# The last product of the last block split by token tile, its output stored in four pieces

## The chip, the cores and the metric

The kernel runs on one core of a Trainium2 chip. The metric is the device time of one execution in microseconds, as the median of several executions. A core has five engines that run side by side and wait for each other by semaphores: PE (TensorE, matrix products, which go to the accumulation memory PSUM), DVE (VectorE, elementwise), ACT (ScalarE, functions and copies), POOL (GpSimd) and SP (SyncE, which here issues the DMA transfers).

## The reference, cut to what matters

The kernel computes a state-space attention block (Mamba-2 SSD, 4 sequences of 768 tokens, 8 heads of 32) and a gated feed-forward network behind it:

```
def _moe_ref(x, w_gate, w_val, w_out, rms_g):      # x: 3072 tokens x 256
    rms = np.sqrt(np.mean(x * x, axis=-1, keepdims=True) + 1e-06)
    xn = x / rms * rms_g
    g = xn @ w_gate                                # 256 x 1536
    silu = g * (1.0 / (1.0 + np.exp(-g)))
    val = xn @ w_val                               # 256 x 1536
    return (silu * val @ w_out).astype(np.float32) # 1536 x 256
```

Its `x` is the attention output, with the heads side by side. The change concerns the last product alone, `silu * val @ w_out`, for the last 512 tokens.

## The kernel before, in words

All is float32. The 3072 tokens go in six blocks of 512 (`TB`, `NBLK`). Blocks 1 to 5 take each matrix product of the network in a Strassen (Winograd) form with seven products of half-size matrices instead of eight. The order of all steps of a block is written out by hand as a list of names with numbers (the strings at the end of the kernel); a loop calls the function of each name. There is one list for block 1, one for blocks 2 to 4 and one for the last block, in which nothing of a next block is prepared. The engines keep the order of this list, each for its own instructions, and wait for each other where data or buffers ask for it.

The output product of a block has a left matrix of 512 tokens x 1536, held turned as six tiles `h` (`j` = 0 to 5, each with two slices of 128 hidden units), and `w_out`. The tokens are split in two halves (`a` = 0, 1) of two token tiles (`t` = 0, 1) of 128 each, in the order that `put_half` shows (`(t a p)`), the 256 output columns in two halves of 128 (`m` = 0, 1). The steps are:

- `O.k.j` (`product_o`, L801 to L817): product k of tile j, two 128x128 matmuls, one per token tile, at L815. Products 1, 6 and 7 add up in one bank, products 5 and 3 in a second, 2 in a third, 4 in a fourth. Products 2 and 5 are in tiles of the tag "val", the others in tiles of the tag "gate", two buffers each. A tile holds both token tiles side by side.
- `s`, `s2`, `s3`, `s4` (L786 to L798): sums and differences of tiles of h on DVE; `s4.j` (L798) makes the left matrix of product 3, `Sh[j]`.
- `Otake.k` (`taken_o`, L827): ACT copies the first bank to the tile `v` after products 1, 6 and 7.
- `Oadd.c` (`total_o`, L829 to L834): DVE adds such a copy and one of the other banks into quarter c of the output tile `ob` (first digit: token half, second: column half). `Oadd.22` reads the second bank when product 5 is in it, `Oadd.12` when product 3 has been added as well.
- `out.a` (`put_half`, L836 to L838): SP stores one token half, 256 rows of 256 columns.

In the last block the list ends with product 3 (`O.3.0` to `O.3.5`), `Oadd.21`, `out.1`, `Oadd.12` and `out.0`: the last store waits for the last addition, and that for the last matmul.

Of the kernel before, what the change touches and what calls it, by code (L numbers as in the profile page):

```python
# [9 lines left out]
FP32 = mybir.dt.float32  # L10
# [5 lines left out]
ALU = mybir.AluOpType  # L16
# [4 lines left out]
def kernel(  # L21
# [33 lines left out]
    nc = tc.nc  # L55

    P = 128
# [5 lines left out]
    DM, DF = moe_w_gate.shape  # L63
    T = NB * S
    NF = DF // P
    NPAIR = T // 256
    TB = 512
    NT = TB // P
    NBLK = T // TB
# [11 lines left out]
    def bank(name, shape):  # L81
        return mm.tile(list(shape), FP32, tag="one", bufs=2, name=name)
# [5 lines left out]
    pairs, later, sides = {}, {}, ("left", "right")  # L88
# [29 lines left out]
    wo = const.tile([P, NF, DM], FP32, name="wo")  # L118
# [573 lines left out]
    def combine_w(j):  # L692
        if j < NF // 4:
            s = raw.tile([P, 2, 4, P], FP32, tag="wr", name="sw", bufs=6)
        else:
            s = const.tile([P, 2, 4, P], FP32, name="sw%d" % j)
        Sw[j] = s
        f1, f2 = slice(2 * j * P, (2 * j + 1) * P), slice((2 * j + 1) * P, (2 * j + 2) * P)
        a11, a12, a21, a22 = wgv[:, :, 0, f1], wgv[:, :, 1, f1], wgv[:, :, 0, f2], wgv[:, :, 1, f2]
        for k, in0, in1, op in ((0, a21, a22, ALU.add), (1, s[:, :, 0], a11, ALU.subtract),  # L700
                                (2, a11, a21, ALU.subtract), (3, a12, s[:, :, 1], ALU.subtract)):
            nc.vector.tensor_tensor(out=s[:, :, k], in0=in0, in1=in1, op=op)
# [66 lines left out]
    two = {}  # L769
# [30 lines left out]

    Os, ts, obs = {}, {}, {}  # L801

    def product_o(blk, k, j):
        bank_of = {1: "X", 6: "X", 7: "X", 2: 2, 4: 4, 5: 5, 3: 5}[k]
        if k in (1, 2, 4, 5) and j == 0:
            val = k in (2, 5)
            Os[bank_of] = later[val].tile([P, 512], FP32, tag="val" if val else "gate",
                                          name="o", bufs=2)
        o = Os[bank_of]
        a11, a12, a21, a22 = tiles_of_h(blk, j)  # L810
        lhsT = {1: a11, 2: a12, 4: a22, 7: a21}[k] if k in (1, 2, 4, 7) else Sh[j]
        rhs = {1: wo[:, 2 * j, 0:P], 2: wo[:, 2 * j + 1, 0:P], 3: wo[:, 2 * j + 1, P:DM],
               **{k: two[j // 2][:, {4: 3, 5: 0, 6: 1, 7: 2}[k], j % 2] for k in (4, 5, 6, 7)}}[k]
        for t in range(2):
            nc.tensor.matmul(out=o[:, t * P:(t + 1) * P], lhsT=lhsT[:, t], rhs=rhs,  # L815
                             start=(k in (1, 2, 4, 5) and j == 0 and t == 0), stop=True,
                             skip_group_check=True)  # L817

    def halves_of(o):
        return o[:, 0:2 * P].rearrange("p (t m) -> p t m", t=2)  # L820
# [5 lines left out]
            ts[k] = ffn.tile([P, 2, P], FP32, tag="v", name="v", bufs=2)  # L826
        nc.scalar.copy(out=ts[k], in_=halves_of(Os["X"]))  # L827

    def total_o(blk, c):  # L829
        if blk not in obs:  # L830
            obs[blk] = ffn.tile([P, 2, 2, DM], FP32, tag="ob", name="ob", bufs=1)
        a, m, v, o = {11: (0, 0, 1, 2), 22: (1, 1, 7, 5), 21: (1, 0, 7, 4), 12: (0, 1, 6, 5)}[c]
        nc.vector.tensor_tensor(out=obs[blk][:, :, a, m * P:(m + 1) * P], in0=ts[v],
                                in1=halves_of(Os[o]), op=ALU.add)  # L834

    def put_half(blk, a):  # L836
        dst = out[blk * TB:(blk + 1) * TB, :].rearrange("(t a p) m -> p t a m", t=2, a=2)
        nc.sync.dma_start(out=dst[:, :, a], in_=obs[blk][:, :, a])  # L838

    def put(blk, k, o, ob):  # L840
        nc.scalar.copy(out=ob, in_=o)
# [154 lines left out]
    def of_chunk(n, fn):  # L996
# [3 lines left out]
        "P": product_gv, "take": taken_gv, "C": total_gv, "silu": silu_gv, "hid": hide_gv,  # L1000
        "s": combine_h, "s3": difference_h, "s2": second_h, "s4": fourth_h,
        "O": product_o, "Otake": taken_o, "Oadd": total_o, "out": put_half,
        "cw": lambda blk, j: combine_w(j) if blk == 1 else None,
        "two": lambda blk, j: combine_wo(j) if blk == 1 else None,
        "turn": of_pair(1, turn), "T": of_pair(1, lambda p, i: turned(p, i, ac.copy)),
# [14 lines left out]
    for blk in range(1, NBLK):  # L1020
# [27 lines left out]
        elif blk < NBLK - 1:  # L1048
            order = """
                P.1.0 load.0 take.1.0 turn.0.1 P.1.1 take.1.1 spread.0 P.6.0 P.2.0 T.0.1  # L1050
                turn.0.0 take.6.0 P.6.1 Tt.0.1.0 Tt.0.1.1 take.6.1 T.0.0 P.7.0 C.11.0 Tt.0.0.0
                P.2.1 P.7.1 take.7.0 C.11.1 P.4.0 P.5.0 Tt.0.0.1 take.7.1 P.4.1 silu.21.0 C.22.0
                silu.21.1 silu.11.1 g.0 silu.22.0 P.5.1 scale.1 hid.21.1 silu.11.0 hid.11.0
                hid.21.0 P.3.0 C.22.1 hid.11.1 P.1.3 L1.0.3 P.1.2 take.1.3 P.3.1 hid.22.0 A.0
                turn.1.1 take.1.2 T.1.1 P.2.2 L1.0.2 P.6.2 P.6.3 C.12.0 C.12.1 L.0 take.6.2 S.0
                P.2.3 take.6.3 C.11.3 turn.1.0 P.7.3 silu.22.1 P.7.2 Tt.1.1.0 silu.12.0 hid.12.0
                hid.22.1 y.0 C.11.2 T.1.0 take.7.3 take.7.2 spread.1 P.5.2 sq.0 silu.12.1 P.5.3
                silu.11.2 hid.12.1 silu.11.3 P.4.3 silu.21.3 C.22.2 Tt.1.1.1 Tt.1.0.0 yt.0
                C.22.3 P.4.2 s.0 hid.21.3 Tt.1.0.1 P.3.2 P.1.5 silu.21.2 hid.11.3 P.3.3 sub.0
                g.1 take.1.5 P.6.5 hid.11.2 silu.22.2 s.1 take.6.5 P.1.4 hid.21.2 C.12.2 C.12.3  # L1060
                P.2.5 P.2.4 silu.22.3 hid.22.3 take.1.4 silu.12.2 L.1 C.11.5 P.7.5 hid.22.2
                take.7.5 s3.0 L1.1.3 silu.12.3 P.6.4 hid.12.3 P.5.5 take.6.4 C.11.4 silu.11.4
                hid.12.2 spread.2 P.4.5 C.22.5 P.5.4 P.7.4 P.3.5 silu.22.5 sub.1 silu.21.5 A.1
                silu.11.5 L1.1.2 take.7.4 C.22.4 S.1 y.1 P.3.4 silu.22.4 s3.1 P.4.4 hid.22.4
                O.5.0 O.1.0 hid.11.5 C.12.5 hid.21.5 silu.21.4 C.12.4 s.2 silu.12.5 O.1.1 O.1.2
                hid.22.5 silu.12.4 hid.12.5 hid.12.4 s.3 O.5.1 scale2.0 sq.1 hid.21.4 O.5.2
                O.2.0 hid.11.4 s2.2 ms s2.1 s2.0 s.4 O.1.3 O.4.0 O.1.4 O.5.3 s.5 s3.3 O.1.5
                O.2.1 mc O.5.4 s2.3 spread.3 mt Otake.1 sub.3 O.6.0 O.2.2 s2.4 s3.2 O.6.1 rs
                O.4.1 O.5.5 O.6.2 O.6.3 load.1 O.6.4 s2.5 O.6.5 s3.4 O.2.3 s4.3 s4.1 s4.0 rb
                O.4.2 Otake.6 O.7.0 O.7.1 O.7.2 s4.4 O.7.3 ex.3 O.2.4 ex.1 s4.5 s3.5 O.7.4 ex.0  # L1070
                O.7.5 O.2.5 yt.1 O.4.3 O.4.4 O.4.5 sub.2 s4.2 Otake.7 Oadd.22 O.3.0 Oadd.21
                table O.3.1 O.3.2 O.3.3 Oadd.11 ex.2 xn O.3.4 O.3.5 tx out.1 Oadd.12 out.0
            """
        else:
            order = """
                P.1.0 take.1.0 P.1.1 take.1.1 P.2.0 P.6.0 P.6.1 take.6.0 P.2.1 take.6.1 C.11.0
                C.11.1 P.7.0 P.7.1 P.5.0 silu.11.1 take.7.1 take.7.0 P.5.1 P.4.0 silu.21.0 P.4.1
                C.22.1 P.3.1 P.1.2 P.1.3 hid.21.0 P.2.2 silu.22.1 silu.21.1 silu.11.0 hid.22.1
                take.1.2 hid.21.1 C.22.0 C.12.1 P.3.0 P.6.2 silu.12.1 take.1.3 hid.11.1 C.11.2
                P.6.3 hid.11.0 C.12.0 take.6.2 take.6.3 silu.22.0 hid.22.0 silu.12.0 P.2.3 P.5.2  # L1080
                P.7.3 C.11.3 hid.12.0 take.7.3 P.7.2 P.5.3 silu.11.2 take.7.2 P.4.3 C.22.2
                silu.21.3 P.4.2 hid.12.1 s.0 P.3.2 silu.21.2 C.22.3 hid.11.2 P.3.3 P.1.5
                silu.22.2 hid.21.3 P.2.5 s.1 take.1.5 silu.22.3 P.1.4 hid.22.2 C.12.2 silu.12.2
                hid.21.2 silu.11.3 C.12.3 P.2.4 take.1.4 P.6.5 silu.12.3 P.6.4 take.6.5 hid.22.3
                C.11.5 hid.11.3 s3.0 P.5.5 C.11.4 hid.12.3 P.7.5 take.6.4 P.7.4 hid.12.2
                take.7.5 take.7.4 P.5.4 C.22.5 s.2 P.3.5 silu.11.5 P.4.4 P.4.5 O.5.0 C.12.5
                hid.11.5 O.5.1 s3.1 C.22.4 O.5.2 s.3 P.3.4 O.4.0 silu.21.5 silu.21.4 hid.21.4
                silu.12.5 silu.11.4 O.5.3 O.1.0 hid.11.4 O.1.1 silu.22.4 O.1.2 O.1.3 O.2.0
                hid.21.5 C.12.4 s2.1 silu.12.4 s2.0 O.2.1 silu.22.5 hid.12.5 s2.2 hid.12.4 O.1.4
                s3.2 hid.22.5 O.4.1 hid.22.4 s.4 O.2.2 O.1.5 s.5 O.5.4 O.4.2 Otake.1 O.5.5 s2.3  # L1090
                O.6.0 s2.5 O.6.1 O.6.2 s2.4 O.6.3 s3.3 s3.5 O.6.4 O.6.5 s3.4 Otake.6 O.2.3 s4.3
                O.4.3 O.7.0 O.7.1 O.7.2 O.4.4 O.7.3 s4.0 O.7.4 s4.5 s4.1 s4.2 O.7.5 Otake.7
                Oadd.22 O.2.4 O.2.5 O.4.5 O.3.0 O.3.1 Oadd.11 s4.4 O.3.2 O.3.3 Oadd.21 O.3.4
                O.3.5 out.1 Oadd.12 out.0
            """
        for step in order.split():
            kind, *numbers = step.split(".")
# [31 lines left out]
```

## Time and profile before

| | |
|---|---|
| median of 5 executions | 418.3 us (417.62 to 418.48) |
| the profiled execution | 417.77 us |
| its span, first to last instruction | 416.1 us |
| PE busy | 410.0 us, 99% of the span |
| DVE busy | 304.2 us, 73% |
| ACT busy | 229.5 us, 55% |
| granted TensorE clock | 1.00 |
| last matmul of the kernel ends | 412.47 us |
| last store issued, landed | 412.96 us, 415.09 us |
| stores of the last block | 2 of 256 KB each |

The profile is one execution, recorded by the hardware. Times in its views count from the start of the span. Lines L... are lines of the kernel. A float32 matmul stands as two records of PE, each with a record of its weight load (PEld). "SPq" and the like are an engine's instruction queue: waits and the issuing of DMAs, which do not count as busy. A DMA has two times: the instruction that issues it, and the landing, when its semaphore tells that all data are written. In the view of groups, the number after "x" is the count, and after the bar stand busy time in us and the mean of one in ns; "<-" in brackets names what ended the engine's wait.

### The profile page before, as it was taken

Reading aid. Unit: us, or ns where it says so; the run is one execution under the profiler, and the core shown is the slowest. Engines: PE = TensorE matmul, PEld = TensorE weight load, DVE = VectorE, ACT = ScalarE, POOL = GpSimd, SP = SyncE. Lnnn points to the kernel's source line nnn. Section 1 sums busy time; section 2 is a strip of 40 time slices with the busy share of each in tenths; the row PEclk is TensorE's granted clock in tenths of the full one; section 3 lists DMA queues with packets and bytes.
Section 4 is the critical chain, followed back from the end, with each engine's and each line's share of the span. In section 5 each row is a group of like instructions: output and inputs, shape, how many; then the busy total and the mean of one; then the engine's idle time right before and its main releaser. Section 6 shows DMA issues by size and latency. Waiting matters only on the chain.

```text
span 416.1 us, 7930 instructions
## 1 busy us (share of the span) xinstructions
PE 410.0 (99%) x3100; PEld 344.5 (83%) x3100; DVE 304.2 (73%) x665; ACT 229.5 (55%) x462; POOL 38.9 (9%) x48
## 2 busy tenths in 40 slices
PE   7999999999999999999999999999999999999996
PEld 4665478888878899888899887899888889988896
DVE  6899998979679886466986476895476684547671
ACT  3998998877656316645328645527646521245410
POOL 3020000013000005000013100014100000000000
PEclk9999999999999999999999999999999999999999
DMA  9989849001007112702070503070100000100001
GB/s 114 230 198 183 229 118 368 4 0 51 1 2 151 43 62 46 107 2 101 20 136 25 77 2 101 2 154 2 51 2 0 2 2 1 52 0 2 0 2 50
DMA packets 86564, 27.99 MB, mean 67 GB/s; under 512 B 76000, under 2 KB 80352, under 8 KB 86528
## 3 DMA queue, kind: packets, MB, share of 16 engines
q1 hardware_dynamic: 82368, 27.24, 28.2%
q10 hardware_dynamic: 4160, 0.26, 0.7%
q8 instruction: 24, 0.39, 0.4%
q14 instruction: 12, 0.10, 0.1%
HBM read 24.22 MB, written 3.28 MB: 66 GB/s over the span
## 4 chain that ended last, share of the span: by engine, by line
PE 98%; DVE 1%; issue 0%; ACT 0%
PE gate L732 28%; PE o L815 23%; PE val L732 21%; PE o L764 5%; PE g L468 4%; PE gate L648 3%; PE y L550 3%; PE y L541 2%; PE tp L434 2%; PE gate L658 2%; PE A_ps L501 1%; PE e L363 1%; PE rb L613 1%; PE idle L266 1%; PE ms L591 1%; PE e L374 1%
## 5 line engine op out<-in xcount | busy, mean ns | idle before, releaser
L744 DVE TENSOR_TENSOR c<-val,p 128x512 f32<-128x512 f32 x99 | 67.3, 686 | 49.8 <-PE val L732 37.7
L738 ACT COPY p<-gate 128x512 f32<-128x512 f32 x99 | 57.7, 587 | 68.2 <-PE gate L732 63.3
L732 PE MATMUL gate<-tx,sw 128*128 128x256 f32 x264 | 65.0, 383 | 0.0
L732 PEld LDWEIGHTS gate<-tx,sw 128*128 128x128 f32 x264 | 48.8, 190 | 8.1 <-issue 2.0
L757 DVE TENSOR_TENSOR h<-c 128x256 f32<-128x256 f32 x99 | 41.0, 432 | 19.0 <-ACT c L753 18.9
L753 ACT ACTIVATE c<-c 128x256 f32<-128x256 f32 x99 | 38.1, 413 | 11.5 <-DVE c L744 10.7
L732 PE MATMUL val<-xn,sw 128*128 128x256 f32 x132 | 34.1, 384 | 0.0
L732 PE MATMUL val<-tx,sw 128*128 128x256 f32 x132 | 33.9, 384 | 0.0
L815 PE MATMUL o<-wo,h 128*128 128x128 f32 x240 | 33.7, 278 | 0.0
L732 PE MATMUL gate<-tx,wgv 128*128 128x256 f32 x132 | 33.1, 381 | 0.0
L732 PE MATMUL val<-xn,wgv 128*128 128x256 f32 x132 | 33.1, 380 | 0.0
L732 PE MATMUL gate<-xn,wgv 128*128 128x256 f32 x132 | 33.0, 381 | 0.0
L815 PE MATMUL o<-two,s 128*128 128x128 f32 x240 | 32.0, 276 | 0.0
L569 POOL TENSOR_TENSOR sq<-sq 128x256 f32<-128x256 f32 x12 | 10.1, 839 | 227.3 <-ACT sq L568 197.2
L815 PE MATMUL o<-two,h 128*128 128x128 f32 x240 | 30.9, 276 | 0.0
L815 PEld LDWEIGHTS o<-wo,h 128*128 128x128 f32 x240 | 29.9, 192 | 1.0 <-issue 0.6
L815 PEld LDWEIGHTS o<-two,s 128*128 128x128 f32 x240 | 29.9, 192 | 0.3
L827 ACT COPY v<-o 128x256 f32<-128x256 f32 x15 | 5.6, 372 | 43.6 <-PE o L815 43.6
L815 PEld LDWEIGHTS o<-two,h 128*128 128x128 f32 x240 | 28.9, 192 | 0.0
L732 PEld LDWEIGHTS val<-tx,sw 128*128 128x128 f32 x132 | 24.6, 190 | 4.5 <-DVE h L757 1.0
L732 PEld LDWEIGHTS val<-xn,sw 128*128 128x128 f32 x132 | 24.5, 190 | 4.1 <-issue 0.7
L732 PEld LDWEIGHTS gate<-tx,wgv 128*128 128x128 f32 x132 | 24.9, 191 | 3.4 <-issue 0.2
(158 smaller groups left out, 697.4 us busy)
## 6 DMA issues: line engine op xcount, KB each, us to landing
L<-rowd SPq DMA_DIRECT2D x16, 512.0 KB, 4.8
xr<-in_x_dram SPq DMA_DIRECT2D x24, 128.0 KB, 3.5
wr<-in_moe_w_out_dram SPq DMA_DIRECT2D x6, 512.0 KB, 6.9
wr<-in_moe_w_gate_dram SPq DMA_DIRECT2D x5, 512.0 KB, 5.7
wr<-in_moe_w_val_dram SPq DMA_DIRECT2D x5, 512.0 KB, 6.1
out_dram<-ob SPq DMA_DIRECT2D x10, 256.0 KB, 2.2
br<-in_B_dram SPq DMA_DIRECT2D x22, 64.0 KB, 4.1
cr<-in_C_dram SPq DMA_DIRECT2D x22, 64.0 KB, 3.3
```

The source lines that it names most:

```text
L434: nc.tensor.transpose(out=tp[:, k], in_=src[:, i].rearrange("p h n -> p (h n)"), identity=ident)
L468: nc.tensor.matmul(out=g[:, 256 * i:256 * i + 256], lhsT=T[r, i, 0], rhs=T[r, i, 1:3].rearrange("p t m -> p (t m)"), start=(i == 0), stop= ...
L550: nc.tensor.matmul(out=y[o:o + 32, h // 4, i * P:(i + 1) * P], lhsT=s["x"][:, i, h], rhs=Ls[p][:, i, h], start=opens, stop=True, tile_posi ...
L569: nc.gpsimd.tensor_tensor(out=sqs[blk][:, tk], in0=sq2[:, 0], in1=sq2[:, 1], op=ALU.add)
L648: nc.tensor.matmul(out=gv[:, k], lhsT=w[:, t, fs], rhs=xns[0][:, t], start=(t == 0), stop=(t == 1))
L732: nc.tensor.matmul(out=dst[:, half[w]], lhsT=lhsT, rhs=rhs, start=(k in (1, 2, 5) and w == 0), stop=True, skip_group_check=True)
L738: nc.scalar.copy(out=t, in_=Xs[j])
L744: nc.vector.tensor_tensor(out=t, in0=Zs[j], in1=a, op=ALU.add)
L753: nc.scalar.activation(out=u, in_=src[:, half[0]], func=AF.Silu)
L757: nc.vector.tensor_tensor(out=hidden_tile(blk, j)[:, c // 10 - 1, c % 10 - 1], in0=u, in1=src[:, half[1]], op=ALU.mult)
L764: nc.tensor.matmul(out=o, lhsT=hs_[blk, f // 2][:, f % 2, k // 2, (k % 2) * P:(k % 2 + 1) * P], rhs=wo[:, f], start=opens, stop=(f == NF - ...
L815: nc.tensor.matmul(out=o[:, t * P:(t + 1) * P], lhsT=lhsT[:, t], rhs=rhs, start=(k in (1, 2, 4, 5) and j == 0 and t == 0), stop=True, skip ...
```

## The change

In the last block, product 5 and 3 go to two single banks (`bank`, two buffers of the tag "one", which the attention stages use), one per token tile, instead of one "val" tile. Product 3 runs all six `j` of the first token tile, then all six of the second. The additions from these banks, `Oadd.22` and `Oadd.12`, become two instructions of 128x128 each, and the second half of product 3 may run while the first is added. The step `s4.4` moves ahead of `Oadd.11` and product 3. The output is stored in four pieces: quarter (0, 0) of 128 KB, half 1 of 256 KB, and quarter (0, 1) in two eighths of 64 KB, whose rows are 512 bytes.

```diff
-    def product_o(blk, k, j):
+    def product_o(blk, k, j, ts=(0, 1)):
         bank_of = {1: "X", 6: "X", 7: "X", 2: 2, 4: 4, 5: 5, 3: 5}[k]
+
+        apart = bank_of == 5 and blk == NBLK - 1
         if k in (1, 2, 4, 5) and j == 0:
             val = k in (2, 5)
-            Os[bank_of] = later[val].tile([P, 512], FP32, tag="val" if val else "gate",
-                                          name="o", bufs=2)
+            if apart:
+                Os[5] = [bank("o", (P, P)) for t in ts]
+            else:
+                Os[bank_of] = later[val].tile([P, 512], FP32, tag="val" if val else "gate",
+                                              name="o", bufs=2)
...
+        for t in ts:
+            nc.tensor.matmul(out=o[t] if apart else o[:, t * P:(t + 1) * P], lhsT=lhsT[:, t],
+                             rhs=rhs, start=(k in (1, 2, 4, 5) and j == 0 and (apart or t == 0)),
+                             stop=True, skip_group_check=True)
+
+    def products_of_t(blk, k, t):
+        for j in range(NF // 2):
+            product_o(blk, k, j, (t,))
...
-    def total_o(blk, c):
+    def total_o(blk, c, ts_=None):
...
+        if isinstance(Os[o], list):
+            for t in (0, 1) if ts_ is None else (ts_,):
+                nc.vector.tensor_tensor(out=obs[blk][:, t, a, m * P:(m + 1) * P], in0=ts[v][:, t],
+                                        in1=Os[o][t], op=ALU.add)
...
+    def put_quarter(blk, a, m, t=None):
+        dst = out[blk * TB:(blk + 1) * TB, :].rearrange("(t a p) m -> p t a m", t=2, a=2)
+        t, ms = slice(0, 2) if t is None else slice(t, t + 1), slice(m * P, (m + 1) * P)
+        nc.sync.dma_start(out=dst[:, t, a, ms], in_=obs[blk][:, t, a, ms])
...
+        "Ot": products_of_t, "quarter": put_quarter,
...
-                Oadd.22 O.2.4 O.2.5 O.4.5 O.3.0 O.3.1 Oadd.11 s4.4 O.3.2 O.3.3 Oadd.21 O.3.4
-                O.3.5 out.1 Oadd.12 out.0
+                Oadd.22 O.2.4 O.2.5 O.4.5 s4.4 Oadd.11 Oadd.21 quarter.0.0 out.1 Ot.3.0
+                Oadd.12.0 Ot.3.1 quarter.0.1.0 Oadd.12.1 quarter.0.1.1
```

More of the change, by code (lines that the diff above doesn't have):

```diff
@@ L811, in product_o @@
         lhsT = {1: a11, 2: a12, 4: a22, 7: a21}[k] if k in (1, 2, 4, 7) else Sh[j]
[L812 to L817, printed above, removed]
+        if k < 4:
+            rhs = wo[:, 2 * j + (k > 1), (k // 3) * P:(k // 3 + 1) * P]
+        else:
+            rhs = two[j // 2][:, {4: 3, 5: 0, 6: 1, 7: 2}[k], j % 2]
+        for t in ts:
[5 more added lines that the diff above has]
+            product_o(blk, k, j, (t,))
     def halves_of(o):
@@ L832, in total_o @@
         a, m, v, o = {11: (0, 0, 1, 2), 22: (1, 1, 7, 5), 21: (1, 0, 7, 4), 12: (0, 1, 6, 5)}[c]
-        nc.vector.tensor_tensor(out=obs[blk][:, :, a, m * P:(m + 1) * P], in0=ts[v],
-                                in1=halves_of(Os[o]), op=ALU.add)
+        if isinstance(Os[o], list):
+            for t in (0, 1) if ts_ is None else (ts_,):
+                nc.vector.tensor_tensor(out=obs[blk][:, t, a, m * P:(m + 1) * P], in0=ts[v][:, t],
+                                        in1=Os[o][t], op=ALU.add)
+        else:
+            nc.vector.tensor_tensor(out=obs[blk][:, :, a, m * P:(m + 1) * P], in0=ts[v],
+                                    in1=halves_of(Os[o]), op=ALU.add)
     def put_half(blk, a):
```

## The prediction

> **What bounds the kernel now.** I read the page first, then the chain of waits, then the order of time over the last microseconds, because the diff touches only the last of the six blocks.
>
> ```profile
> span 416.1 us, 7930 instructions
> ...
> PE   7999999999999999999999999999999999999996
> ...
> PE 98%; DVE 1%; issue 0%; ACT 0%
> ```
>
> PE (TensorE) is full in every slice from the second to the one before the last, and 98% of the chain is PE. So work of other engines counts only where PE has nothing left to do: at the very end. The chain from 390 us on shows where that is:
>
> ```profile
> 395.06 17.43 PE o L815 x156
> 412.49 0.02 issue
> 412.51 0.42 DVE ob L833
> ```
>
> After 412.47 us PE is done. What is left, 3.6 us of the 416.1 us span, is one addition, one store and the program's closing. The order of time, 398 to 417 us, has the steps that the change touches (columns: start, duration, engine, line, operation):
>
> ```profile
> 408.49 0.37 ACT L827 COPY v<-o 128x256 f32<-128x256 f32 x1 [3.65 <-PE o L815]
> 408.90 0.91 DVE L833 TENSOR_TENSOR ob<-v,o 128x256 f32<-128x256 f32 x2 [3.33 <-ACT v L827]
> ...
> 409.63 2.84 PE L815 MATMUL o<-wo,s 128*128 128x128 f32 x24
> 409.72 0.42 DVE L798 TENSOR_TENSOR s<-h,s 128x256 f32<-128x256 f32 x1
> 410.06 0.41 DVE L833 TENSOR_TENSOR ob<-v,o 128x256 f32<-128x256 f32 x1
> 410.50 2.83 SPq L838 DMA_DIRECT2D out_dram<-ob  x2
> 412.51 0.42 DVE L833 TENSOR_TENSOR ob<-v,o 128x256 f32<-128x256 f32 x1 [2.04 <-PE o L815]
> ```
>
> The 24 PE records at 409.63 are the last product (O.3.0 to O.3.5: twelve 128x128 float32 matmuls, two records each). The last record runs 0.276 us, so records start every (2.84 - 0.276)/23 = 0.111 us. DVE then adds Oadd.12 (412.51 to 412.93), SP issues the last store at 412.96, and its DMA is seen in slices of 0.2 us (last two columns: DMA share, GB/s):
>
> ```profile
> 413.50:413.70 0.20, 0.00 (x0) 0.00 (x0) 0.00 (x0) 0.00 (x0) 0.00 (x0) 1.00 0.00 0
> 413.70:413.90 0.20, 0.00 (x0) 0.00 (x0) 0.00 (x0) 0.00 (x0) 0.00 (x0) 1.00 0.11 41
> 413.90:414.10 0.20, 0.00 (x0) 0.00 (x0) 0.00 (x0) 0.00 (x0) 0.00 (x0) 1.00 1.01 358
> ...
> 414.50:414.70 0.20, 0.00 (x0) 0.00 (x0) 0.00 (x0) 0.00 (x0) 0.00 (x0) 1.00 0.64 215
> 414.70:414.90 0.20, 0.00 (x0) 0.00 (x0) 0.00 (x0) 0.00 (x0) 0.00 (x0) 1.00 0.01 0
> ```
>
> From the trace's records of this store: first packet 413.85, last 414.74, last landing 415.09. So it took 0.89 us before data, 0.89 of data, 0.35 to landing: 2.13 in all. From landing to the end of the span is 0.97 us, in which SP goes on through its closing waits:
>
> ```profile
> L1124 SPq EVENT_SEMAPHORE  x3: 28/28/28, 415.1 to 415.2; - x3
> L1124 SPq DRAIN  x2: 7/7/7, 415.3 to 415.4; - x2
> ```
>
> **PE: the same work, in another order.** The twelve matmuls stay twelve, now six for the first 128 tokens (t=0), then six for t=1; each already loaded weights of its own. At 0.111 us a record, t=0 ends at 409.63 + 11 x 0.111 + 0.276 = 411.13 and t=1 at 412.47 as before. Cost 0. Two covers stand behind this. First, t=0 needs the last fourth_h (s4.4) after 8 records instead of 16, at 410.52. On DVE, Oadd.22 becomes two additions of 0.28 us from 408.90, done by about 409.5, and s4.4 now stands ahead of Oadd.11, so it ends by 409.9: 0.6 us to spare. Second, the first matmul of the product waits for the first half of Oadd.22, done at about 409.2, and PE gets there at 409.63. Products 5 and 3 leave the "val" buffers for the two single banks that the earlier stages used, so product 2 now takes the buffer that product 5 had, and waits for a product of PE 25 matmuls earlier, long past. PE has no gap in that stretch (10.00 of 10 us busy from 380 to 390 and from 390 to 400), so no wait there can be won, and only a new one lost: 0.
>
> **DVE: the last addition is half as wide.** For the price I go by groups with shapes kept apart (columns after the bar: busy us, mean ns):
>
> ```profile
> L833 DVE TENSOR_TENSOR ob<-v,o 128x256 f32<-128x256 f32 x20 | 8.0, 417 | 18.5 <-ACT v L827 12.4 <-PE o L815 6.0
> ...
> L513 DVE TENSOR_TENSOR A<-A_ps,tmask 128x128 f32<-128x128 f32 x8 | 2.3, 284 | 0.0
> ```
>
> L513 is a tensor_tensor from PSUM of just 128x128: 0.284 us against this addition's 0.421. Gain 0.14 us (bounds: 0.08 by L912's 0.341 us, 0.21 if it were half). The first half, Oadd.12.0, runs at 411.17 to 411.45, from another bank than the one PE then writes, beside PE. The two more DVE instructions all lie beside PE.
>
> **The last store is a quarter as large.** Four stores take the place of two: 128 KB issued about 410.25 (after Oadd.11), 256 KB about 410.65 (after Oadd.21), 64 KB about 411.5, and the last 64 KB at 412.96 - 0.14 = 412.82. One issue holds SP 0.37 us, so SP is free from about 411.9 and the last issue waits for DVE alone. By the 0.89 to first data, the earlier three begin at 411.1, 411.5 and 412.4 and move 448 KB; at the 350 GB/s of the slices above that is 1.3 us, done by about 412.7, a microsecond before the last one's data. They cost nothing. If that cover were gone, the last would queue behind 64 KB, 0.2 to 0.4 us. For the last store the DMA view has (median to landing):
>
> ```profile
> out_dram<-ob SPq DMA_DIRECT2D x10, 256.0 KB, 2.2
> ...
> out_dram<-ob SPq DMA_DIRECT2D x4, 128.0 KB, 1.8
> ...
> rowd<-r_sb SPq DMA_DIRECT2D x2, 64.0 KB, 3.6
> ```
>
> The first of the four 128 KB stores (100.33) found the queue empty: first packet after 0.84, landed after 1.73. Its 1 KB packets take 46 ns, 8 on each of 16 engines. The row of the right shape is rowd's: 64 KB in 512-byte packets of 27 ns, but landed after 2.1 and 5.1 us among the weight loads (DMA share 94% from 58.0 us). So: 0.84 to the first packet; 8 x 0.027 = 0.22 of data, plus the 0.17 that the engines' starts lie apart in the present store (0.89 less 16 x 0.045); 0.35 to landing; 1.58 us. Check: 1.73 - 8 x 0.019 = 1.58. Gain 2.13 - 1.58 = 0.55. Bounds: 0 by rowd's 2.1; 0.80 if two more halvings bring together twice what the first did (2.13 - 1.73 = 0.40). I take 0.55, since the 128 KB row is of the same tile, to the same tensor, with nothing before it.
>
> Against splitting speaks the Trainium skill, "DMA: Bandwidth & Descriptors": its section Bandwidth wants transfers of a megabyte and calls those under 64 KB dominated by descriptors, and its section on the anatomy of one DMA gives about 2.0 us fixed (for the GpSimd path) plus the bytes at 436 GB/s. By that formula 192 KB less saves an estimated 0.44 us, and the sum below would be 0.71 instead of 0.82; the 128 KB row's 1.73 us already lies under its fixed part.
>
> **The closing waits.** SP ends with five waits of two semaphores each. Stores take the eight DMA semaphores in turn. The present last store has the sixth, which stands in the third wait: after landing, two more waits of 0.063 us follow (415.10, 415.17, 415.23, then the drain at 415.29). With two stores more, the last has the eighth, in the fifth wait, and the four before it are over by then. Gain 0.13 (bounds 0 and 0.13).
>
> **Sum.** 0.14 + 0.55 + 0.13 = 0.82 us. The profiled execution took 417.77 us, 1.7 us of it outside its span: 416.95. It is one of the faster of five (417.62 to 418.48); from their median of 418.3 I forecast 417.5.
>
> **Rivals.**
> - The fixed part of a store is all that counts. For it: rowd's 2.1 us. Against it: 1.73 for half the bytes. Then only 0.27 us is won: 418.0. The same holds roughly where the change does less than it says because the third store still occupies the engines (0.55 less 0.3). Chance 0.10.
> - The small store gains more, 0.80, by a shorter way to landing as well: 1.07 us in all, 417.2. For it: packets shrink in number and size. Against it: the 0.35 us is the same or longer (0.38) for the 128 KB store. Chance 0.14.
> - Slower: six matmuls in a row that add to the same 128 columns of one bank. Before, t=0 and t=1 alternate, so ten boundaries in the last product are new. If the next record must wait for the end of the one before, each costs 0.276 - 0.111 = 0.165 us, 1.65 together; with a whole record more, 2.76. That outweighs the 0.82 from 0.08 us a boundary on. In the middle (2.2), 1.4 is lost: 419.7. Against it: the two records of one matmul add to the same columns now, and start 0.111 us apart. Chance 0.06.
> - The forecast itself, 0.6 to 1.0 us won (417.3 to 417.7): 0.70.
>
> **How the numbers follow.** 0.2% is 0.84 us, about what a measurement of this kernel can tell from no change, and my sum of 0.82 stands on that bound. I split the forecast's chance 0.38 beyond and 0.32 within it, a little more beyond, because the median of the 256 KB stores is 2.2 us and this one took 2.13: an execution with the usual store wins a little more. Faster: 0.38 + 0.14 = 0.52; within: 0.32 + 0.10 = 0.42; slower 0.06. The range takes in the first two rivals and a spread of some 0.2 us between medians: 417.0 to 418.1.
>
> **What would show it.** The 24 records of the last product must still take 2.84 us with no gap in the middle, and s4.4 end before 410.5. The last two additions must last 0.28 us each, 1.3 us apart. The last store must show its first packet 0.84 us after issue, 0.4 us of data and landing within 1.6; the closing drain must follow the landing by 0.08 instead of 0.21 us. I am wrong if that store lands after 2.1 us, or if PE's end moves past 412.5.

## The result, and the profile after

| | before | changed |
|---|---|---|
| median (executions) | 417.79 us (46) | 416.95 us (26) |
| lowest and highest | 417.51, 418.66 | 416.64, 417.61 |
| profiled execution, its span | 417.77, 416.1 us | 416.92, 415.2 us |
| end of PE to end of span ("the tail") | 3.58 us | 2.73 us |

The changed kernel is faster: ratio 0.9977, 95% interval 0.9972 to 0.9983, which is 0.7 to 1.2 us. The forecast gain was 0.82 us and the medians lie 0.84 us apart, but the forecast time of 417.5 and its range from 417.0 miss 416.95. The five executions shown with the kernel before had a median of 418.3; all 46 have 417.79.

The changed kernel's page, its size and its chain of waits:

```profile
span 415.2 us, 7936 instructions
...
PE 98%; DVE 1%; issue 0%; ACT 0%
```

PE bounds it as before. The order of time, 396 to 416 us:

```profile
408.89 0.48 DVE L846 TENSOR_TENSOR ob<-v,o 128x128 f32<-128x128 f32 x2 [3.33 <-ACT v L838]
...
409.30 0.42 DVE L798 TENSOR_TENSOR s<-h,s 128x256 f32<-128x256 f32 x1
...
409.63 2.84 PE L822 MATMUL o<-wo,s 128*128 128x128 f32 x24
409.63 0.74 DVE L849 TENSOR_TENSOR ob<-v,o 128x256 f32<-128x256 f32 x2
410.07 0.37 SPq L859 DMA_DIRECT2D out_dram<-ob  x1
410.54 0.42 SPq L854 DMA_DIRECT2D out_dram<-ob  x1
411.17 0.29 DVE L846 TENSOR_TENSOR ob<-v,o 128x128 f32<-128x128 f32 x1 [0.79 <-PE o L822]
411.49 1.68 SPq L859 DMA_DIRECT2D out_dram<-ob  x2
412.51 0.29 DVE L846 TENSOR_TENSOR ob<-v,o 128x128 f32<-128x128 f32 x1 [1.05 <-PE o L822]
```

Line for line: the 24 PE records stand at 409.63 and last 2.84 us, as before. s4.4 (L798) is done by 409.72. The first token tile is added at 411.17, while PE works on the second, and the last addition starts at the same 412.51 as before, but lasts 0.29 us instead of 0.42. The last store in slices of 0.2 us (last columns: DMA share, GB/s), and SP's closing:

```profile
413.40:413.60 0.20, 0.00 (x0) 0.00 (x0) 0.00 (x0) 0.00 (x0) 0.00 (x0) 1.00 0.00 0
413.60:413.80 0.20, 0.00 (x0) 0.00 (x0) 0.00 (x0) 0.00 (x0) 0.00 (x0) 1.00 0.48 148
413.80:414.00 0.20, 0.00 (x0) 0.00 (x0) 0.00 (x0) 0.00 (x0) 0.00 (x0) 1.00 0.62 180
414.00:414.20 0.20, 0.00 (x0) 0.00 (x0) 0.00 (x0) 0.00 (x0) 0.00 (x0) 1.00 0.00 0
```

```profile
L1146 SPq EVENT_SEMAPHORE  x5: 27/28/28, 413.2 to 414.4; - x5
L1146 SPq DRAIN  x2: 7/7/7, 414.4 to 414.5; - x2
```

Data flow in two slices where there were five. Of the five closing waits only the last is after the landing (414.37 in the trace's records), and the drain follows 0.08 us behind the landing. The steps of the tail, from the records (us):

| | before | changed | gain |
|---|---|---|---|
| last addition | 0.421 | 0.286 | 0.135 |
| last store, issue to first packet | 0.886 | 0.846 | 0.040 |
| first to last packet | 0.889 | 0.341 | 0.548 |
| last packet to landing | 0.351 | 0.356 | -0.005 |
| landing to drain | 0.208 | 0.081 | 0.127 |
| rest of the tail | 0.826 | 0.818 | 0.008 |

### The profile page after: what moved, and what is told of

It is laid out like the page before. It is cut to its first block, busy times and chain, and to the rows that moved or that the text cites. A ratio compares the mean times of both kernels' runs of the same rounds, so it can differ in the third digit from the quotient of the medians.

```text
span 415.2 us, 7936 instructions
## 1 busy us (share of the span) xinstructions
PE 410.2 (99%) x3100; PEld 344.5 (83%) x3100; DVE 304.3 (73%) x667; ACT 229.6 (55%) x462; POOL 38.9 (9%) x48
## 4 chain that ended last, share of the span: by engine, by line
PE 98%; DVE 1%; issue 0%; ACT 0%
PE gate L732 28%; PE o L822 23%; PE val L732 21%; PE o L764 5%; PE g L468 4%; PE gate L648 3%; PE y L550 3%; PE y L541 2%; PE tp L434 2%; PE gate L658 2%; PE A_ps L501 1%; PE e L363 1%; PE rb L613 1%; PE idle L266 1%; PE ms L591 1%; PE e L374 1%
```

## The experiments: which part brings what

My theory was the sum of the prediction: addition, size of the last store, place in the closing waits. The rivals: the store's cost is fixed and the earlier product brings the gain, or the closing waits cost nothing. The tail of one profile tells these apart better than medians, whose scatter is told further down. The tail repeats: three profiles of the kernel before have 3.58 us, two of the changed kernel 2.73, and two more with the same end but fewer idle matmuls at the start (further down) 2.74.

**Stores alone.** The product, its tiles and the additions as before (`put_quarter` as in the change):

```diff
...
-                O.3.5 out.1 Oadd.12 out.0
+                O.3.5 quarter.0.0 out.1 Oadd.12 quarter.0.1
```

> The kernel before, with its product and additions as they were; only the stores of the last block differ: quarter (0,0) of 128 KB, half 1 of 256 KB, then quarter (0,1) of 128 KB as the last. Measure: the tail, from the end of PE (412.47 us) to the end of the span; 3.58 us before, 2.73 us after. My theory (a store's time falls with the bytes and rows it carries, and the place of its semaphore in the closing waits counts): the last addition stays at 0.42 us, the last store lands 1.73 us after issue instead of 2.13, and as it has the seventh DMA semaphore, one closing wait of 0.063 us less follows. Tail 3.58 - 0.40 - 0.06 = 3.12 us, median 0.46 us under before. Rival (a store has a fixed cost, what counted was the earlier product): store 2.1 us, tail 3.52 us, median 0.06 us under before.

Measured: tail 3.19 us, median 417.42, ratio 0.9991 (0.9982 to 0.9999). The store landed after 1.81 us instead of the expected 1.73: its 128 KB go in 256 rows of 512 bytes, where the row I took from had 128 rows of 1 KB. Half the bytes in the same number of rows took 0.31 us off the store (2.126 to 1.812 in the records), so the rival with a fixed cost (tail 3.52) is out.

**Product and additions alone.** The changed kernel with the two stores of before:

```diff
-                Oadd.22 O.2.4 O.2.5 O.4.5 s4.4 Oadd.11 Oadd.21 quarter.0.0 out.1 Ot.3.0
-                Oadd.12.0 Ot.3.1 quarter.0.1.0 Oadd.12.1 quarter.0.1.1
+                Oadd.22 O.2.4 O.2.5 O.4.5 s4.4 Oadd.11 Oadd.21 out.1 Ot.3.0
+                Oadd.12.0 Ot.3.1 Oadd.12.1 out.0
```

> The changed kernel with the two stores of before (half 1, then half 0 of 256 KB behind the last addition): the product by token tile and the split additions alone. My theory: only the last addition's 0.42 us becomes 0.29, the store is the old one (2.13 us) with the sixth semaphore: tail 3.58 - 0.135 = 3.45 us, median 0.13 us under before. Rival (the order of the product brings most): tail under 3.2 us, median 0.4 us or more under before.

Measured: tail 3.44 us, median 418.11, ratio 1.000 (0.9991 to 1.0008). Order and split additions together bring 0.14 us of the tail by themselves, the shorter last addition. The medians don't show it: 417.82 for the kernel before in the same series, and seven of this run's eleven executions were of the slower of two groups (further down).

**The place in the closing waits.** The changed kernel with block 0's four stores joined in pairs, so that the last store has the sixth DMA semaphore again:

```diff
     for k in range(NT):
-        put(0, k, ps["o"][:, k % 2, k // 2], ob[:, k])
+        nc.scalar.copy(out=ob[:, k], in_=ps["o"][:, k % 2, k // 2])
+        if k % 2:
+            nc.sync.dma_start(out=out[(k - 1) * P:(k + 1) * P, :].rearrange("(k p) m -> p k m", k=2),
+                              in_=ob[:, k - 1:k + 1])
```

> The changed kernel, but block 0 stores its output, 300 us earlier, in two transfers of 256 KB instead of four of 128 KB. Nothing at the end changes but which of the eight DMA semaphores the last store gets: the sixth, as before the change, instead of the eighth. My theory: two closing waits of 0.063 us follow the landing again: tail 2.73 + 0.13 = 2.86 us, median 0.13 us over the changed kernel. Rival (the place in the closing waits costs nothing, the drain waits for something else): tail 2.73 us.

Measured: tail 2.87 us, 0.14 more than the changed kernel; from landing to drain 0.21 us as before the change. The rival is out. The place is chance: it depends on the number of transfers in the whole program. The median, 417.54 with a ratio of 0.9987 (0.9978 to 0.9996), lies higher than this accounts for; so does the profiled execution, 417.86 us, whose PE ended at 413.29. This led to the question further down.

**The old order with the small stores.** Both token tiles of one j, then the next:

```diff
-                Oadd.22 O.2.4 O.2.5 O.4.5 s4.4 Oadd.11 Oadd.21 quarter.0.0 out.1 Ot.3.0
-                Oadd.12.0 Ot.3.1 quarter.0.1.0 Oadd.12.1 quarter.0.1.1
+                Oadd.22 O.2.4 O.2.5 O.4.5 s4.4 Oadd.11 Oadd.21 quarter.0.0 out.1 O.3.0 O.3.1
+                O.3.2 O.3.3 O.3.4 O.3.5 Oadd.12.0 quarter.0.1.0 Oadd.12.1 quarter.0.1.1
```

> The changed kernel with its two banks, additions and four stores, but product 3 in the old order (both token tiles of one j, then the next j). The first token tile is then ready two records (0.22 us) before the end instead of 1.34 us. My theory: the additions end as late as in the changed kernel, but the two stores of 64 KB are issued behind each other; SP needs 0.43 us from one issue to the next, so the last one goes out at 412.61 + 0.43 = 413.04 instead of 412.82: tail 2.73 + 0.22 = 2.95 us, median 0.2 us over the changed kernel. Rival (the last store's size is all that counts): tail 2.73 us, no difference.

Measured: tail 2.99 us, median 417.21, ratio 0.9986 (0.9977 to 0.9995). Its order of time, 409.5 to 417 us:

```profile
409.67 2.84 PE L822 MATMUL o<-wo,s 128*128 128x128 f32 x24
...
412.33 0.51 DVE L846 TENSOR_TENSOR ob<-v,o 128x128 f32<-128x128 f32 x2 [1.91 <-PE o L822]
412.64 0.82 SPq L859 DMA_DIRECT2D out_dram<-ob  x2
```

Both additions end as early behind PE's end as in the changed kernel (0.33 us), but SP issues the stores one behind the other, the last at 413.08 in the records, 0.25 us late. So the shorter addition comes from the split into two, which the old order allows as well. Running the token tiles one after the other is worth 0.25 us beside the small stores, because the first of them is then issued long before the last.

## The experiments: why the executions scatter

The 46 executions before the change form two groups, 25 at 417.51 to 417.80 and 21 at 418.24 to 418.66; of the changed kernel's 26, 17 lie at 416.64 to 416.96 and 9 at 417.39 to 417.61. Group by group the medians are 417.77 and 416.92, 418.32 and 417.42: 0.85 and 0.90 us apart. Of the five executions behind my base, three were of the upper group. The profile of the run with joined stores was the first of that group; the records of its PE part from the changed kernel's at 5.5 us. PE's order of time there, first the changed kernel's:

```profile
5.51 0.67 PE L304 MATMUL r_ps<-mids,la 128*128 128x256 f32 x2 [0.16 <-ACT la L283]
6.02 0.49 PE L339 MATMUL full_ps<-la,ones 128*128 128x192 f32 x2
6.34 0.59 PE L363 MATMUL e<-never,ident 128*128 128x512 bf16 x2
```

and that of the run with joined stores:

```profile
5.51 1.19 PE L304 MATMUL r_ps<-mids,la 128*128 128x256 f32 x2
6.49 0.85 PE L339 MATMUL full_ps<-la,ones 128*128 128x192 f32 x2
7.13 1.06 PE L363 MATMUL e<-never,ident 128*128 128x512 bf16 x2
```

The same matmuls take nearly twice as long. In every profile PE starts at half pace (an idle matmul of 256 columns takes 0.213 us from start to start; of 512 columns it is 0.43 us at half pace, later 0.22) and doubles once; in the run with joined stores that is at 10.3 us, in the changed kernel's profile at 5.0. The clock column shows 1.00 for both, so it doesn't tell. The next runs asked whether this sets the time: the kernel before twice more, the changed kernel once more, and the changed kernel with 6 and with 9 instead of 12 idle matmuls at the start:

```diff
-    for k in range(12):
+    for k in range(6):
         nc.tensor.matmul(out=idle[:, 0, 0:256], lhsT=warm[:, 0:P], rhs=warm, start=True, stop=True)
```

> The changed kernel with 6 instead of 12 of the idle matmuls at its start (their result is used by nothing). What it asks: why executions of one kernel fall into groups some 0.5 us apart (before 417.5 to 417.8 and 418.2 to 418.7; changed 416.6 to 417.0 and 417.4 to 417.6). My theory: at the start PE runs at half pace (an idle matmul of 256 columns every 0.213 us) until it has been busy for one whole period that starts at a random time; in the changed kernel's profile the pace doubles at 5.0 us, in that of the run e3 only at 10.3 us, and its PE ends 0.81 us later. With a hole from 2.4 to 3.7 us in PE's work the early doubling cannot happen: no execution under 417.2 us, median 417.6 or more, doubling at 7 us or later in the profile. Rival (the groups come from the loads or from outside the kernel): the low group stays, about half or more of the executions at 416.6 to 417.0, median 417.0.

> The kernel before, unchanged, for a second profile. My theory (the time of an execution is set by when PE's pace doubles): PE's end and the time lie together, 412.5 us and 417.6 to 417.8 if the pace doubles by 5.5 us, 413 us or later and 418.2 to 418.7 if it doubles at 7 us or later; the tail is 3.58 us either way. Rival (the groups lie in the tail or before the first matmul): PE's end minus the pace's doubling tells nothing, the tail differs.

> The kernel before, unchanged, for a third profile; the same expectations as for the second.

> The changed kernel with 9 idle matmuls at its start instead of 12. With 6, PE's first real work (the transposes aT) started at 3.26 us, when its data had landed, instead of 3.78 us behind the twelfth idle matmul, though the pace doubled only at 7.7 us. My theory (both the start of aT and the time of the doubling set PE's end): with 9 the idle work ends at 3.0 us, aT starts at 3.26 us, and the hole is small enough for the pace to double at 4 to 5.5 us in many executions; those take 0.3 to 0.5 us less than the changed kernel's 416.6 to 417.0, so 416.2 to 416.6 us, and the median lies 0.2 to 0.5 us under the changed kernel in the same job. Rival (PE is bound later in the start, by the loads, so that the earlier aT is lost again): median as the changed kernel's, within 0.1 us.

> The changed kernel, unchanged, as the control in the same job: the tail 2.73 us, executions at 416.6 to 417.0 and 417.4 to 417.6; PE's end by the time of the doubling as in the profiles so far (4.0 us: 412.3; 4.7 to 5.4 us: 412.5; 10.3 us: 413.3).

The time of the doubling is worked out from the records, to within some 0.1 us:

| profile | pace doubles | PE's first transposes | PE ends | profiled execution |
|---|---|---|---|---|
| before, second and third | 4.03, 4.12 us | 3.78 us | 412.29, 412.34 us | 417.58, 417.63 us |
| before, first | 4.67 | 3.78 | 412.47 | 417.77 |
| changed, first | 5.0 | 3.78 | 412.47 | 416.92 |
| changed, stores joined | 10.33 | 3.78 | 413.29 | 417.86 |
| changed, again | 10.37 | 3.78 | 413.28 | 417.72 |
| changed, last store from ACT (further down) | 10.15 | 3.78 | 413.19 | 417.67 |
| changed, 6 idle matmuls | 7.9 | 3.26 | 412.39 | 416.84 |
| changed, 9 idle matmuls | 9.42 | 3.23 | 412.53 | 416.99 |

In the rows with the first transposes at 3.78 us a late doubling goes with a late end of PE, 413.2 to 413.3 instead of 412.3 to 412.5 us; the five other profiles with 12 idle matmuls fit (doubling at 4.0 to 5.4 us, PE's end at 412.31 to 412.53). The delay is there as soon as both have doubled: the same transposes (L434) start at 10.07 us in the changed kernel's profile and at 10.87 with joined stores, 0.80 us later, and PE's end is 0.81 us later. The tail of all three profiles of the kernel before is 3.58 us. So this scatter comes from the first ten microseconds, and not from the stores or from anything that the change touches. Two things stay open. The three profiles of the kernel before all doubled early, so its upper group was expected to be late but was not seen in a profile. And the late profiles, at 417.67 to 417.86 us, lie above the 417.39 to 417.61 of the changed kernel's first series; where the pace doubles in those executions isn't known.

My expectation of the run with 6 idle matmuls fell. I expected no execution under 417.2 us; all eight lay at 416.84 to 417.44, seven of them under it, median 417.03, ratio 0.9973 (0.9963 to 0.9984). PE's order of time, 1 to 9 us, tells why:

```profile
1.11 1.46 PE L266 MATMUL idle<-warm 128*128 128x256 bf16 x6 [1.11 <-DVE warm L191]
3.26 0.81 PE L270 MATMUL aT<-ident,a_sb 32*128 32x32 f32 x6 [0.69 <-DMA a_sb<-in_a_dram]
...
4.96 1.19 PE L304 MATMUL r_ps<-mids,la 128*128 128x256 f32 x2
```

The doubling is late, as expected, but the twelve idle matmuls had held PE until 3.78 us, and without six of them the transposes start when their data land, 0.52 us earlier. That pays for the late doubling. So the numbers of the rival came, half of the executions at 417.0 or less and a median of 417.0, but not for its reason: the profile shows the late doubling together with the earlier start. With 9 of them the eleven executions took 416.79 to 417.47, median 416.99, ratio 0.9976 (0.9967 to 0.9985); the changed kernel itself, measured beside it, 416.64 to 417.78, median 417.43, ratio 0.9979 (0.9970 to 0.9988). The intervals overlap, so no version is shown to be faster; the expected 416.2 to 416.6 did not come. What the profiles show is that at a doubling as late as 9.4 to 10.4 us PE ends 0.75 us earlier with 9 than with 12. Of this 0.58 us is there before the doubling (L328's first record starts at 9.36 and 9.94 us); the rest goes with the earlier doubling. The fastest executions are no faster.

The Trainium skill, "TensorE: Matmul & The Clock Gate", section "Part 1: The HAM clock gate", tells of half clock until the array has been busy for one window of 3.4 us, with windows that run free of the kernel's start. The change of the doubling from execution to execution agrees with it. By its windows the doubling should come by 1.1 + 2 x 3.4 = 7.9 us, an estimate by that page; three profiles with 12 idle matmuls had it at 10.15 to 10.37 us, though PE had nearly no gap. What counts as busy there no run here shows.

## The experiments: a store split over two queues

To shorten the store once more, the last 64 KB went as two stores of 64 partitions each (two of block 0's stores are joined as well, not shown):

```diff
-        nc.sync.dma_start(out=dst[:, t, a, ms], in_=obs[blk][:, t, a, ms])
+        if t != slice(1, 2):
+            nc.sync.dma_start(out=dst[:, t, a, ms], in_=obs[blk][:, t, a, ms])
+            return
+        for q, r in ((nc.sync, slice(0, 64)), (nc.scalar, slice(64, P))):
+            q.dma_start(out=dst[r, t, a, ms], in_=obs[blk][r, t, a, ms])
...
```

> The changed kernel with its last store of 64 KB in two of 32 KB (64 partitions each) from SP and from ACT, issued at the same time; of block 0's four stores two are joined, so that the two have the seventh and eighth DMA semaphores. My theory (after the issue there is 0.85 us to the first packet, whatever the size, 0.34 of data on the same 16 DMA engines, 0.36 to landing): nothing is gained beyond 0.05 us, tail 2.70 to 2.75 us. Rival (half the rows in each store again shorten it as from 256 to 128 KB): tail 2.55 us.

Both theories fell: tail 3.37 us, which takes back some 0.65 of the 0.85 us. The median of 418.06, ratio 0.9999 (0.9990 to 1.0008), shows no gain at all, but seven of its eleven executions were of the upper group. The first packet came after 1.20 us, and ACT's store landed after 2.1. Two more kernels asked whether ACT's queue or the two at once were to blame: in the first ACT issues the whole store, in the second SP issues both halves.

> The changed kernel with its whole last store of 64 KB issued by ACT instead of SP. In the run e6 two stores of 32 KB, one from SP and one from ACT at the same time, had their first packet after 1.20 us instead of 0.85, the tail was 3.37 us. Theory A (ACT's queue, not used since the start of the kernel, takes longer to begin): first packet about 1.2 us after issue, landing about 2 us after issue, tail over 3.1 us. Theory B (two issues at the same time are in each other's way): first packet after 0.85 us, tail 2.73 us as in the changed kernel.

> The run e6 with both stores of 32 KB issued by SP, one behind the other. Theory A (ACT's queue is slow to begin): the first store's first packet 0.85 us after its issue, the second is issued about 0.43 us later and lands about 1.55 us after its own issue: tail 2.73 + 0.43 = 3.16 us or a little less. Theory B (two stores in flight at once hinder each other): first packet of the first store later than 1.0 us, tail 3.4 us or more.

From ACT alone the whole store has its first packet after 0.88 us and lands after 1.57; the tail is 2.77 us. So ACT's queue is not slow. With both halves from SP the first has its first packet after 1.20 us and lands after 1.85, the second lands after 1.88; the tail is 3.67 us. The issue itself differs, in the view of the issuing line of the run with two queues (durations in ns):

```profile
L863 SPq DMA_DIRECT2D out_dram<-ob x1: 553/553/553, 412.7 to 412.7; - x1
L863 ACTq DMA_DIRECT2D out_dram<-ob x1: 575/575/575, 412.7 to 412.7; - x1
```

Each takes 0.55 us or more where the 128-partition store takes 0.345. That holds for the first of two issued in turn as well, and its issue (412.73 to 413.28 us) was over before the second began at 413.33, so the longer issue goes with the 64-partition form and not with two stores meeting. But it is 0.20 us of the 0.35 by which the first packet is late. The signs that I had named for theory B in this run (first packet later than 1.0 us, tail 3.4 us or more) came, so that two stores in flight hinder each other is not ruled out. A single store of 64 partitions with nothing behind it wasn't tried; what makes the rest stays open.

## Why the prediction was right in its steps and wrong in its number

- **PE at no cost**: right. The 24 records take 2.84 us as before, s4.4 ended at 409.72 (expected 409.9), and the two profiles' PE ends at the same 412.47. That the ends agree to the hundredth is partly luck, as PE's end scatters from 412.29 to 413.29; the 2.84 us are the evidence. The slower rival (sums in a row to the same columns) is out: the 24 records start 0.111 to 0.112 us apart throughout, as before.
- **Addition 0.14**: 0.135.
- **Store 0.55, from 2.13 to 1.58**: 0.58, to 1.54. The sum over packets held; the data took 0.34 instead of 0.39. The row of the right size (rowd's 2.1 us) would have misled, since it lay among the weight loads. The estimate by the formula of the Trainium skill ("DMA: Bandwidth & Descriptors", section "Anatomy of one DMA — SWDGE (gpsimd) path"), 0.44 for the bytes (0.45 with KB of 1024), was short by 0.14. The warning of the same page's section "Bandwidth" against transfers under 64 KB had no price at 64 KB, which landed soonest of all; the stores of 32 KB did take longer, 1.85 us and more.
- **Closing waits 0.13**: 0.127, and 0.14 when the place was undone by itself.
- **The cover of the earlier stores**: the third landed at 413.06, before the last one's first packet at 413.67.
- **Sum 0.82**: the span fell by 0.85, the medians by 0.84. That both medians lie in the lower of their groups (25 of 46, 17 of 26) is chance.

The step that failed is "from their median of 418.3 I forecast 417.5". The sum was sound, the base was not: against the 417.79 of all executions it gives 416.97, and 416.95 was measured. What 417.5 describes is the upper group, which went from 418.32 to 417.42. And the range had "a spread of some 0.2 us between medians": in five values from two groups 0.55 us apart, one more value of the other group moves the median by nearly that much. The five values showed the gap (417.62, 417.77, then 418.30), and I took it for scatter around one middle. Taken from the profiled execution instead, which was of the lower group, the same sum gave 416.95, as the prediction says on its way.

## What to carry to other kernels

When an engine is full to the end, the program's end is a chain of its own: last result, last store, closing waits. Make the last result and its store as small as the work allows, let all others go out earlier, and price a small store by packets and a row from a quiet stretch, not by a row of the same size from a busy one. Look at the single values behind a median before building on it: where they fall into groups, forecast the groups.

## What the runs showed of the hardware

- A store of 64 KB in 128 rows landed 1.54 us after issue, 128 KB in 256 rows of 512 bytes after 1.81, 256 KB in 1 KB rows after 2.13. Of this 0.85 to 0.89 lie before the first packet and 0.35 to 0.36 after the last. Two stores of 64 rows (32 KB) took 1.85 to 2.1 each.
- The order of the closing waits costs 0.063 us for each wait behind the one that ends last.
- The pace of PE doubles between 4.0 and 10.4 us after the start, differently from execution to execution, and moves PE's end in this kernel by up to 1.0 us (412.29 to 413.29), more than the change itself.
